# Reordering one product, one conversion, the value loads and one solve step in the first pass of a DeltaNet and maxout kernel

## The chip, the cores and the metric

The kernel runs on one core of a Trainium2 chip. The metric is the device time of one execution in microseconds (us); less is better. Besides the times there is one profiled execution, from which the trace and its page come. The engines are called as the page does: PE is TensorE (PEld its weight loads), DVE is VectorE, ACT is ScalarE, POOL is GpSimd, and SP only issues DMAs.

## What is computed

The reference has two layers. The first is the delta rule over 4 batches, 8 heads, 768 tokens and 48 dimensions; the second is a feed-forward layer that takes the maximum of three products.

```python
for t in range(S):                       # first layer; k_n are normalized keys
    kt, vt, bt = (k_n[:, :, t], v[:, :, t], beta[:, :, t, None])
    y[:, :, t] = np.einsum('bhd,bhde->bhe', q[:, :, t], state)
    v_old = np.einsum('bhde,bhd->bhe', state, kt)
    state = state + bt[:, :, :, None] * np.einsum('bhd,bhe->bhde', kt, vt - v_old)
...
h = np.maximum(np.maximum(x @ w1, x @ w2), x @ w3)   # second layer, x is y as 3072 x 384
return (h @ w_out).astype(np.float32)
```

The weights arrive as 64-bit words and are converted to 32-bit floats on the chip.

## The kernel before

**Tiles and stages.** The 768 tokens are cut into 12 chunks of 64. A chunk `c` consists of two units `n = 2c` and `2c + 1`, which hold two batches each. Two chunks make a group `m`, and a group is 512 rows of the feed-forward layer. For each group the kernel solves a triangular system (on VectorE), runs the recurrence of its two chunks (small matmuls on TensorE with copies between them), and puts the outcome through the feed-forward layer (large matmuls on TensorE). The feed-forward layer of group `m` is a generator, `ffn(m)` (L915), and work for the next groups is woven in between its steps.

**The order is written by hand.** Scheduling is manual (L96), so each engine does its instructions in the order in which the Python code issues them, and each DMA queue is in order too. The change concerns the loop over `ffn(0)` (L1141). Step `i` of this generator is one product of three matmuls with a hidden tile; the body of the loop then issues what belongs behind step `i`. Steps 0 to 17 are 256 columns wide (three tiles `f` in two halves, three products each), steps 18 to 26 are 512 wide, and steps 27 to 30 are the output products L958. In each three steps, the first is copied to `h` by ScalarE (L934), and the other two are joined to it by a maximum on VectorE (L940). These evictions free the two PSUM buffers `ffn` that the products take in turn.

**Pieces that the change touches**, with their short names in the tables `FIRST` (L1097) and `EARLY_LINKS` (L1090):

- `P4` to `P7` are key-query products of units 4 to 7: `gram(n, (1,))` (L427). The matmuls L438 fill one of three PSUM buffers called `two`, and a mask L422 on VectorE takes the outcome into `pt`.
- `z0`, `z1` are `join_z` (L702) for chunks 2 and 3 when called at i = 18: matmuls L709 and four copies L712 and L714 on ScalarE into `z`. `j0`, `j1` are `join_u` (L716): matmuls L723 that read `z`, and negated copies L683 into `ut`. `u0` is `new` (L762): matmuls L768 that read `ut` and the values. Their PSUM tiles come from the same three buffers `two`.
- `y1`, `s1` at i = 5 and 6 are the output and the state of chunk 1: on VectorE an addition L812 into `y` and an addition L798 into `st`. `T4` to `T7` turn query tiles on TensorE (L361), and `x1` turns `y`.
- `some(solving, n)` issues n steps of the triangular solve of group 1; a step is a multiplication L565 and a subtraction L569 on VectorE, with up to 256 elements a partition.
- `some(conv, 1)` issues one call of the weight conversion (L221): three operations on ScalarE (L238 to L240) for one piece, and for the piece of the call before a shift on VectorE (L250) and an addition on GpSimd (L254). Two buffers `mant` and `up` are taken in turn, so ScalarE's conversion waits for the addition of two pieces before. `fetch` (L211) loads the pieces, and `less_first` (L880) takes one set of weights from the two others (L883).
- `load_v(c)` (L136) loads the values of a chunk with two DMAs on SP's queue into one of three buffers; `prep_values(c)` (L292) scales them in place on GpSimd (L287). `old_k` (L747) later subtracts a product from them (L752). `load_q(n)` (L133) loads a query tile into one of three buffers with two DMAs.

At i = 16 and 17 units 10 and 11 write their key products to DRAM over GpSimd's queue (`at_d`, L468), and at i = 18 they are read back as `x_bl` (L515) for the solve of group 2, which begins at i = 20.

Of the kernel before, what the change touches and what calls it, by code (L numbers as in the profile page):

```python
# [23 lines left out]
def kernel(  # L24
# [84 lines left out]
    def rows(bb):  # L109
        return slice(C * bb, C * (bb + 1))  # L110
# [19 lines left out]
    def load_k(n, queues=one_queue):  # L130
        load(k, kpad[place(n)], n, queues)

    def load_q(n, queues=one_queue):  # L133
        load(q, qpad[n % NQ], n, queues)

    def load_v(c, queue=nc.sync):  # L136
        vts[c] = work.tile([128, 2, H, D], FP32, name="v_t", bufs=3)
        for bb in range(2):
            queue.dma_start(  # L139
                out=vts[c][rows(bb)].rearrange("p g h d -> p (g h) d"),  # L140
                in_=v[2 * bb : 2 * bb + 2, :, c * C : (c + 1) * C, :].rearrange(
                    "b h p d -> p (b h) d"
                ),
            )
# [66 lines left out]
    def fetch(queue=nc.scalar):  # L211
        if fetched[0] < len(pieces):
            _, src, (a, b) = pieces[fetched[0]]
            st = work.tile([128, 2 * 384], U32, name="w_bits", bufs=5)
            queue.dma_start(
                out=st.rearrange("p (a b) -> p a b", a=a), in_=src
            )
            staged.append(st)
            fetched[0] += 1
# [66 lines left out]
    def scale(c, nrm):  # L286
        nc.gpsimd.tensor_tensor(  # L287
            out=vts[c], in0=vts[c],
            in1=nrm[:, :, :, None].to_broadcast([128, 2, H, D]), op=ALU.mult,
        )  # L290

    def prep_values(c):  # L292

        if c in nrms:
            scale(c, nrms.pop(c))
# [84 lines left out]
    def load_blocks(n, queue=nc.gpsimd):  # L380
        c, g = divmod(n, 2)
        for i in range(2):
            if n % 4 == 2:
                t = kmore[i].rearrange("p a h d -> p (a h d)")[:, 0 : 2 * TURNED]
                t = t.rearrange("p (b x) -> p b x", b=2)
            else:
                t = work.tile(
                    [128, 2, TURNED], FP32, name="turned", tag="w_bits", bufs=5
                )
            turned[n, i] = t  # L390
            nc.gpsimd.memset(t[:, :, TURNED - 48 : TURNED], 0.0)  # L391
            for bb in range(2):
                for par in range(2):
                    for db in range(2):
                        p0, at = DP * par + 32 * db, 32 * (1 - db)
                        (queue, nc.gpsimd)[i].dma_start(  # L396
                            out=t[p0 : p0 + 32, bb, at : at + NP * 2 * D].rearrange(
                                "p (j x) -> p j x", j=NP
                            ),
                            in_=(k, q)[i][  # L400
                                2 * bb + g, :, c * C : (c + 1) * C, :
                            ].rearrange(
                                "(j two) (r tb) d -> two r j (tb d)", two=2, tb=2
                            )[par],
                        )
# [104 lines left out]
    def blocks(m):  # L510
        if m == 1:
            xs[m] = in_wo(0)
        else:
            xs[m] = work.tile([128, 2, HB * BL + HB], FP32, name="x_bl", bufs=1)
        nc.sync.dma_start(  # L515
            out=in_rows(xs[m]),
            in_=at_d[m].rearrange("c f b h j i -> (c f b h) j i"),
        )
# [361 lines left out]
    def less_first(f):  # L880
        part = (slice(None), slice(None), slice(f * 128, (f + 1) * 128))
        for i in (1, 2):
            nc.vector.tensor_tensor(  # L883
                out=w_sb[i][part], in0=w_sb[i][part], in1=w_sb[0][part],
                op=ALU.subtract,
            )

    def turn_first(fs):
        p_f = ps_two("p_t")
        for i, f in enumerate(fs):  # L890
            for t in range(KT):
                nc.tensor.transpose(
                    p_f[:, i, t * 128 : (t + 1) * 128],
                    w_sb[0][:, t, f * 128 : (f + 1) * 128],
                    ident,
                )
        for i, f in enumerate(fs):
            nc.scalar.copy(
                w_sb[0][:, :, f * 128 : (f + 1) * 128],
                p_f[:, i, 0 : KT * 128].rearrange("p (t x) -> p t x", t=KT),  # L900
            )
# [70 lines left out]
    def some(gen, n):  # L972
        for _ in range(n):
            if next(gen, gen) is gen:
                break

    conv = weights()
    solving = solve(0)
# [96 lines left out]
    for n in (2, 3):  # L1075
        masked(pts[n], by_par(pts[n]))
    load_q(4)
    load_v(2)
    solving = solve(1)
    some(solving, 1)  # L1080

# [15 lines left out]
    FIRST = {  # L1097
        0: "f1 s0 S1 S1", 1: "z1 d1 S1 k1 S1 S1", 2: "j1 S1 S1 S1",
        3: "S1 q1 S1 S1", 4: "u1 T4", 5: "y1", 6: "s1 T5", 7: "x1 T6",
        8: "T7", 14: "P4", 15: "P5", 21: "P6", 22: "P7",  # L1100
    }


# [11 lines left out]
    def links(m, names):  # L1115
        for name in names.split():
            f, i = name[0], int(name[1])
            if f in RECURS and m < GROUPS:
                RECURS[f](2 * m + i)
            elif f in MADE and m + 1 < GROUPS:  # L1120
                MADE[f](2 * (m + 1) + i)
            elif f in UNIT and m + 1 < GROUPS:
                UNIT[f](4 * (m + 1) + i)
            elif f == "N" and m + 2 < GROUPS:
                load_blocks(4 * (m + 2) + i)

    def queries(names):
        for name in names.split():
            f, n = name[0], int(name[1])
            if f not in OF_KEYS:  # L1130
                links(0, name)
                continue
            OF_KEYS[f](n)
            if f == "T" and n + 3 < 11:
                load_q(n + 3)
# [3 lines left out]
    CONVERTED = {*range(6), *range(11, 25)}  # L1139
    FETCHED = {8: 1, 12: 1, 13: 1, 14: 1, 18: 2, 19: 2, 20: 1, 21: 1}  # L1140
    for i, _ in enumerate(ffn(0)):  # L1141
        if 0 < i < 7:
            fetch(nc.sync)
        for _ in range(FETCHED.get(i, 0)):
            fetch(nc.gpsimd)
        if i in (18, 25):
            some(conv, 1)
        if i == 20:
            solving = solve(2)
            some(solving, 1)  # L1150
        if i == 21:
            some(solving, 3)
        queries(FIRST.get(i, ""))
        links(1, EARLY_LINKS.get(i, ""))
        if i in CONVERTED and i != 18:
            some(conv, 1)
        if 3 < i < 14:
            some(solving, (2, 1, 2, 2, 3, 3, 3, 3, 2, 2)[i - 4])
        if i in (5, 7):
            prep_values(i // 2)  # L1160
        if i in (1, 7):
            for n in range(2):
                load_k(8 + 2 * (i > 1) + n, (nc.gpsimd, nc.gpsimd))
        if i == 0:
            load_v(3)
        if i in (0, 2):
            load_q(5 + i // 2)
        if i == 11:
            load_q(11, (nc.gpsimd, nc.gpsimd))
        if i in (10, 21):  # L1170
            load_v(4 + i // 21)
        if i == 18:
            blocks(2)
        if i == 23:
            prep_values(4)
        if i > 21:
            some(solving, (3, 2, 3, 2, 2, 5, 5, 5, 4)[i - 22])
        if i in (27, 28, 29):
            load_blocks(i - 15, nc.sync)
        if i in (15, 17, 19, 22, 25, 27):  # L1180
            less_first((15, 17, 19, 22, 25, 27).index(i))
        if 27 <= i < 30:
            turn_first((2 * (i - 27), 2 * (i - 27) + 1))
# [5 lines left out]
    for m in range(1, GROUPS):  # L1189
        for i, _ in enumerate(ffn(m)):  # L1190
# [4 lines left out]
            if m + 2 < GROUPS:  # L1195
                if i == 6:
                    blocks(m + 2)
                if i == 8:
                    solving = solve(m + 2)
# [32 lines left out]
```

## Time and profile before

| what | us |
|---|---|
| median of 3 runs (lowest, highest) | 525.5 (524.5, 526.3) |
| profiled execution | 524.22 |
| its span, from first to last instruction | 522.5 |

The profiled execution is thus 1.7 us longer than its span. The granted clock of TensorE was 0.966 of full speed on the mean. Busy time by stretch of the span, in us (the engines work side by side, so the rows don't add up):

| stretch | what runs | PE | DVE | ACT | POOL | PE clock |
|---|---|---|---|---|---|---|
| 50 to 65 | i = 0 to 2 | 12.03 | 13.88 | 7.98 | 3.29 | 0.75 |
| 65 to 80 | i = 3 to 7 | 13.83 | 14.52 | 11.10 | 9.14 | 1.00 |
| 80 to 92 | i = 8 to 11 | 10.60 | 11.32 | 3.70 | 5.31 | 1.00 |
| 92 to 102 | i = 12 to 15 | 10.00 | 9.43 | 7.18 | 5.98 | 1.00 |
| 102 to 117 | i = 16 to 19 | 13.24 | 14.01 | 11.39 | 12.30 | 1.00 |
| 117 to 150 | i = 20 to 26 | 33.00 | 30.24 | 16.62 | 15.93 | 1.00 |
| 200 to 350 | later passes | 149.66 | 99.64 | 34.79 | 77.97 | 1.00 |

A stretch in which an engine is busy for its whole length is one that this engine may set the pace of. Short instructions leave a few hundredths of a microsecond between them, so 14.5 of 15 us on VectorE is as good as full.

### The profile page before, as it was taken

To read this page: it belongs to the slowest core of one execution; us is meant where nothing else is said; L and a number is where in the kernel's file an instruction comes from. 1 tells how busy PE (TensorE), PEld (TensorE's weight loads), DVE (VectorE), ACT (ScalarE), POOL (GpSimd) and SP (SyncE) were. 2 spreads that over 40 slices of the span, in tenths; PEclk is the share of its full clock that TensorE was granted. 3 is DMA by queue.
4 is the path that set the end of the run, shared out by engine and by line. 5 is a ranking of instruction groups with operands and counts; after the bars stand their busy time and mean duration, and the time that the engine had idled before them with its cause. 6 is when DMAs were issued, how large, how long until landed. Compare 5 with 4: busy or idle time off the path is not lost.

```text
span 522.5 us, 18030 instructions
## 1 busy us (share of the span) xinstructions
PE 495.1 (95%) x7840; PEld 305.9 (59%) x7840; DVE 311.0 (60%) x695; ACT 164.4 (31%) x302; POOL 190.6 (36%) x314
## 2 busy tenths in 40 slices
PE   6667898989999999999999999999999999999996
PEld 6556686855666555665556565655655555554453
DVE  5876999998995441699652988645897221111100
ACT  5557473776513142200143200242101411011000
POOL 7515155684383844951394780502130000000000
PEclk9855899999999999999999999999999999999999
DMA  8974958476035953444585444823343202220011
GB/s 111 214 154 114 162 163 138 133 154 199 3 89 135 188 90 69 135 125 115 111 157 121 111 131 102 171 43 91 81 109 85 43 3 63 61 61 0 0 30 32
DMA packets 108671, 53.47 MB, mean 102 GB/s; under 512 B 91760, under 2 KB 102928, under 8 KB 108592
## 3 DMA queue, kind: packets, MB, share of 16 engines
q1 hardware_dynamic: 97840, 34.44, 32.3%
q0 software_dynamic: 8640, 17.49, 13.5%
q8 instruction: 62, 1.02, 0.9%
q10 hardware_dynamic: 2112, 0.39, 0.5%
q14 instruction: 17, 0.14, 0.1%
HBM read 39.17 MB, written 13.11 MB: 100 GB/s over the span
## 4 chain that ended last, share of the span: by engine, by line
PE 79%; DVE 12%; ACT 2%; DMA 2%; issue 1%; POOL 1%; SPq 1%; DVEq 0%; ACTq 0%; POOLq 0%
PE p_h L926 34%; PE p_o L958 26%; PE p_g L438 3%; DVE tmp L565 3%; PE p_m L906 2%; PE p_u L768 2%; PE p_y L810 2%; DVE wo_sb L569 2%; DMA kmore<-in_k_dram 2%; PE p_k L740 2%; PE p_j L723 2%; PE p_s L791 1%; PE p_q L740 1%; SPq L120 1%; PE p_z L709 1%
## 5 line engine op out<-in xcount | busy, mean ns | idle before, releaser
L926 PE MATMUL p_h<-xt,w_sb 128*128 128x512 f32 (+1 forms) x522 | 218.9, 564 | 2.8 <-DVE h L940 1.3
L926 PEld LDWEIGHTS p_h<-xt,w_sb 128*128 128x128 f32 x522 | 96.1, 193 | 88.2 <-issue 79.5
L958 PE MATMUL p_o<-wo_sb,h 128*128 128x384 f32 x288 | 97.8, 489 | 0.0
L940 DVE TENSOR_TENSOR h<-h,p_h 128x512 f32<-128x512 f32 (+1 forms) x48 | 29.6, 617 | 90.0 <-PE p_h L926 89.9
L958 PEld LDWEIGHTS p_o<-wo_sb,h 128*128 128x128 f32 x288 | 53.7, 190 | 35.7 <-issue 0.5
L565 DVE TENSOR_TENSOR tmp<-x_bl,y_bl 128x31 f32<-128x31 f32 (+20 forms) x139 | 51.7, 372 | 4.1
L964 ACT COPY o_sb<-p_o 128x384 f32<-128x384 f32 x24 | 11.5, 479 | 134.2 <-PE p_o L958 128.1
L569 DVE TENSOR_TENSOR y_bl<-y_bl,tmp 128x31 f32<-128x31 f32 (+20 forms) x139 | 48.5, 349 | 4.8
L936 ACT ACTIVATE h<-p_h 128x512 f32<-128x512 f32 x30 | 17.9, 597 | 87.7 <-PE p_h L926 84.8
L958 PE MATMUL p_o<-w_sb,xt 128*128 128x384 f32 x120 | 42.0, 486 | 0.0
L396 POOL DMA_DIRECT2D turned<-in_q_dram x72 | 39.1, 551 | 3.9 <-POOL turned L391 2.9
L438 PE MATMUL p_g<-kqt 48*64 48x64 f32 (+1 forms) x1216 | 27.5, 239 | 6.8 <-DVE nt_bl L263 3.8
L438 PEld LDWEIGHTS p_g<-kqt 48*64 48x64 f32 x1216 | 24.3, 139 | 14.8 <-ACT kqt L367 8.0
L958 PEld LDWEIGHTS p_o<-w_sb,xt 128*128 128x128 f32 x120 | 22.8, 190 | 15.9
L120 POOL DMA_DIRECT2D kpad<-in_k_dram x32 | 21.8, 689 | 15.8 <-PE p_s L791 14.3
L287 POOL TENSOR_TENSOR v_t<-v_t,nrm 128x768 f32<-128x768 f32 x12 | 18.2, 1518 | 24.9 <-DVE nrm L266 12.1
L254 POOL TENSOR_TENSOR w_sb<-mant,up 128x384 int32<-128x384 int32 x18 | 18.3, 1018 | 24.3 <-DVE mant L250 21.7
L798 DVE TENSOR_TENSOR st<-st,p_s 48x768 f32<-48x768 f32 (+1 forms) x18 | 17.1, 949 | 15.0 <-PE p_s L791 14.8
L422 DVE TENSOR_TENSOR pt<-p_g,mask 128x512 f32<-128x512 f32 x20 | 13.7, 688 | 15.8 <-PE p_g L438 15.8
L139 POOL DMA_DIRECT2D v_t<-in_v_dram x12 | 9.9, 827 | 35.9 <-PE p_u L768 35.9
L391 POOL MEMSET turned<- 128x96 f32 x18 | 3.3, 191 | 44.8 <-DVE kqt L412 44.8
L768 PEld LDWEIGHTS p_u<-v_t,ut 64*64 64x64 f32 x768 | 13.5, 141 | 7.8 <-issue 7.3
(153 smaller groups left out, 624.5 us busy)
## 6 DMA issues: line engine op xcount, KB each, us to landing
w_bits<-in_moe_w_dram SPq DMA_DIRECT2D x14, 384.0 KB
out_dram<-o_sb SPq DMA_DIRECT2D x48, 96.0 KB
turned<-in_q_dram POOLq DMA_DIRECT2D x72, 48.0 KB, 2.9
kpad<-in_k_dram POOLq DMA_DIRECT2D x32, 96.0 KB, 4.9
y_x<-y SPq DMA_DIRECT2D x16, 192.0 KB
qall<-y_x SPq DMA_DIRECT2D x32, 96.0 KB
ut<-y_d SPq DMA_DIRECT2D x40, 64.0 KB
v_t<-in_v_dram SPq DMA_DIRECT2D x12, 192.0 KB
```

What stands on the lines that cost most here:

```text
L120: queues[bb].dma_start(out=dst[rows(bb ^ g), :, 0:D], in_=src[2 * bb + g, :, c * C : (c + 1) * C, :].rearrange("h p d -> p h d"),)
L254: nc.gpsimd.tensor_tensor(out=dst.bitcast(I32), in0=mant_v.bitcast(I32), in1=up_v, op=ALU.add)
L287: nc.gpsimd.tensor_tensor(out=vts[c], in0=vts[c], in1=nrm[:, :, :, None].to_broadcast([128, 2, H, D]), op=ALU.mult,)
L396: (queue, nc.gpsimd)[i].dma_start(out=t[p0 : p0 + 32, bb, at : at + NP * 2 * D].rearrange("p (j x) -> p j x", j=NP), in_=(k, q)[i][2 * bb ...
L438: nc.tensor.matmul(p_g[rows(bb ^ (g * i)), par, c0 : c0 + C * (1 + whole)], kq[:, 0], kq if whole else kq[:, i],)
L565: nc.vector.tensor_tensor(out=t_v, in0=row.to_broadcast(t_v.shape), in1=column.to_broadcast(t_v.shape), op=ALU.mult,)
L569: nc.vector.tensor_tensor(out=rest, in0=rest, in1=t_v, op=ALU.subtract)
L768: nc.tensor.matmul(p_v[rows(bb ^ g), g, i], ut[c % NU][rows(bb), g, h], rhs[rows(bb), g, h],)
L926: nc.tensor.matmul(p_h, w_sb[i][:, t, f * 128 : (f + 1) * 128], xt[:, t, lo : lo + w], start=(t == 0), stop=(t == KT - 1),)
L936: nc.scalar.activation(out=h, in_=p_h, func=mybir.ActivationFunctionType.Relu)
L940: nc.vector.tensor_tensor(out=h, in0=h, in1=p_h, op=ALU.max)
L958: nc.tensor.matmul(p_o, stays, moves, start=(n == 0), stop=(n == len(terms) - 1))
```

## The change

Four places of the loop over `ffn(0)` and the lines ahead of it are edited:

1. The key-query product of unit 5, `P5`, is issued at i = 19 (ahead of `j0`) and no longer at i = 15.
2. The conversion call of i = 18 is issued behind the links of that step (`d0 d1 z0 z1`) and no longer ahead of them.
3. The values of chunks 2 and 3 are loaded at i = 3 and i = 8 and no longer ahead of the loop and at i = 0; they are scaled at i = 8 and 12 and no longer at i = 5 and 7. The query tiles of units 5 and 6 are loaded at i = 1 and 3 and no longer at i = 0 and 2.
4. At i = 4 one step of the solve is issued and no longer two, and at i = 11 four and no longer three. So from i = 5 to i = 11 each output, state and eviction on VectorE stands one solve step further ahead.

No instruction is added or removed.

```diff
     load_q(4)
-    load_v(2)
     solving = solve(1)
...
-        8: "T7", 14: "P4", 15: "P5", 21: "P6", 22: "P7",
+        8: "T7", 14: "P4", 19: "P5", 21: "P6", 22: "P7",
...
-        if i in (18, 25):
+        if i == 25:
             some(conv, 1)
...
         queries(FIRST.get(i, ""))
         links(1, EARLY_LINKS.get(i, ""))
-        if i in CONVERTED and i != 18:
+        if i in CONVERTED:
             some(conv, 1)
         if 3 < i < 14:
-            some(solving, (2, 1, 2, 2, 3, 3, 3, 3, 2, 2)[i - 4])
-        if i in (5, 7):
-            prep_values(i // 2)
+            some(solving, (1, 1, 2, 2, 3, 3, 3, 4, 2, 2)[i - 4])
+        if i in (8, 12):
+            prep_values(i // 4)
...
-        if i == 0:
-            load_v(3)
-        if i in (0, 2):
+        if i in (1, 3):
             load_q(5 + i // 2)
         if i == 11:
             load_q(11, (nc.gpsimd, nc.gpsimd))
-        if i in (10, 21):
-            load_v(4 + i // 21)
+        if i in (3, 8, 10, 21):
+            load_v((3, 8, 10, 21).index(i) + 2)
```

## The prediction

> **What bounds the kernel now.** I read the page first (parts 1 and 2), then the chain of waits from 50 to 125 us, then the timelines of the engines over the same stretch. All of the change lies in the first feed-forward pass (i = 0 at 51 us to i = 30 at 166 us) and in the loads issued just ahead of it.
>
> ```profile
> PE 495.1 (95%) x7840; PEld 305.9 (59%) x7840; DVE 311.0 (60%) x695; ACT 164.4 (31%) x302; POOL 190.6 (36%) x314
> ...
> PE   6667898989999999999999999999999999999996
> ...
> DVE  5876999998995441699652988645897221111100
> ```
>
> A slice is 13 us. From slice 9 on TensorE is at nine tenths or more, so any microsecond that it gains before about 117 us should reach the end, unless a later wait takes it. Before that VectorE is the full one. The chain of waits (start, us, what) shows where it changes hands:
>
> ```profile
> 77.81 1.11 DVE wo_sb L569
> 78.92 0.86 DVE st L798
> 79.78 0.76 DVE tmp L565
> ...
> 80.56 1.59 DVE wo_sb L569
> ...
> 91.23 0.43 DVE h L940
> ...
> 91.71 1.56 PE p_h L926 x6
> ...
> 113.08 1.02 POOL w_sb L254
> 114.12 0.56 ACT mant L238
> ...
> 115.70 0.42 ACT z L712
> 116.15 0.59 ACT z L714
> ...
> 116.78 0.74 PE p_j L723 x49
> ```
>
> Three stretches: VectorE alone from 50.3 to 91.7; TensorE from 91.7 to 101.8; then a relay of VectorE, GpSimd's `at_d` writes, one weight addition (L254), one conversion on ScalarE (L238 to L240) and only then the copies of z, which release the joins on TensorE. TensorE's timeline shows the price as idle time in brackets:
>
> ```profile
> 60.05 0.21 PE L709 MATMUL p_z<-ut,at 32*32 32x32 f32 x1 [1.93 <-issue]
> 79.83 0.65 PE L361 MATMUL p_t<-ident,qall 128*128 128x128 f32 x4 [1.17 <-DVE st L798]
> 83.54 1.53 PE L926 MATMUL p_h<-xt,w_sb 128*128 128x256 f32 x6 [1.32 <-DVE h L940]
> 116.17 0.24 PE L723 MATMUL p_j<-z,t 32*32 32x32 f32 x2 [1.36 <-ACT z L712]
> 116.78 0.74 PE L723 MATMUL p_j<-z,t 32*32 32x32 f32 x62 [0.36 <-ACT z L714]
> ```
>
> The last four sum to 4.21 us, the most that these edits can reach. The first, 1.93 us, lies where VectorE is full and sets the pace: gaining it gives nothing.
>
> **What the Trainium skill says.** "SBUF — State Buffer", section "Who interferes with whom": a VectorE instruction with two SBUF inputs contends with a GpSimd instruction that reads SBUF, and the loser blocks for the whole instruction. The trace agrees. While GpSimd scales values,
>
> ```profile
> 78.60 3.27 POOL L287 TENSOR_TENSOR v_t<-v_t,nrm 128x768 f32<-128x768 f32 x2
> ```
>
> the pair of the 255-element step takes 0.83 and 1.58 us where a pair three steps on takes 0.42 and 0.42, while the state addition L798, one of whose inputs is PSUM, keeps 0.94 us. "Runtime: NRT & Kernel Launch", section "Instruction fetch mechanics": an engine's program comes in 16 KiB blocks over its own DMA queue; the page here has 62 packets and 1.02 MB on the instruction queue, so 16 KB each. One falls into 57 to 58 us, with the DMA engines at their fullest, beside the 1.93 us stall. "TensorE: Matmul & The Clock Gate", section "What's actually happening": an idle window brings half clock. Here the granted clock is 0.66 from 60.2 to 65.2 us, after that stall.
>
> **Part 1, values later and one solve step later (i = 4 to 12).** The step that leaves i = 4 and comes back at i = 11 puts the output L812 and the state L798 each one step earlier on VectorE: 0.42 + 0.42 us and two gaps of 0.02, 0.87 us. So the state ends about 0.87 sooner, of which the turn at 79.83 can use all: its gap of 1.17 falls to 0.3. Next, h L940 at 82.98 follows two further steps; without the scaling they lose 0.41 + 1.16 = 1.57 us of blocking. It would end near 81.0 and not 83.39, and TensorE, free at 81.3 by then, has no gap: 2.1 us ahead.
>
> But VectorE remains the bound. At i = 8 one scaling (1.65 us in the trace when it contends) now follows GpSimd's four kpad loads (2.73 us) and one weight fetch (0.78), so near 81.1 to 82.8, and meets solve steps. Not shown there; bound: nothing if it falls on a PSUM operation, 1.2 us (the larger block above) otherwise. I take 1.15, as VectorE does little else than steps then. Up to the eviction that ended at 91.65 VectorE is thus ahead by one step (192 elements, 0.36 + 0.36 + 0.05 = 0.77) + 1.57 - 1.15 = 1.2 us. TensorE's 2.1 is cut to 1.2.
>
> The step is paid back before the eviction at 98.64 to 99.05, which frees the buffer of the product of i = 15; that one started at 99.55, 0.5 us later. VectorE's lead there is 1.57 - 1.15 = 0.42, so TensorE's is at most 0.92. The second scaling at i = 12 comes behind the addition of 97.67 to 98.67; what follows on VectorE is one eviction and two masks from PSUM, which it does not block, and a `mant` shift (0.35, seen at up to 1.41 us when blocked). The next eviction has 3 us in hand, so I charge nothing; without that cover it is 1.1. Part 1: **0.9 us** (0 to 2.1).
>
> The loads themselves: the two value loads (two DMAs of 192 KB each) and two query loads move back on SP's queue. SP goes in order, so the weight fetches of i = 1 to 3 come ahead of them and the query load of i = 3 waits for the buffer that the third fetch waits for (until about 68.8). The query tiles are turned at 76 and 79.8, the values scaled at 81 and 98: the slack is 5 us or more. On GpSimd the kpad loads leave 3.3 us sooner. Cost nothing. The second scaling lands in GpSimd's densest stretch: 94 to 107.5 has 4.3 us idle (the brackets of its timeline), 2.27 of it in one piece ahead of the `at_d` writes, so 1.65 fits.
>
> **Part 2, key-query product from i = 15 to 19.** 32 matmuls, 0.69 us, and one mask of 0.68 us. On TensorE moved, not removed; it makes everything between 101 and 115 us 0.69 earlier and now fills the place ahead of the joins. The mask leaves the start of the relay at 101.80; the next shift waits for ScalarE until 102.4, so the relay gains little more than part 1's 0.42.
>
> **Part 3, conversion behind the copies of z (i = 18).** Before, ScalarE copied the hidden tile (112.29 to 112.88), waited 1.25 us for GpSimd's addition, converted for 1.5 us (114.12 to 115.6), then copied z in four pieces of 0.58. After, z follows the hidden copy. The relay up to there gains 0.4, so the first two copies end near 113.6. TensorE arrives: product of i = 19 ended at 114.81; less 0.92 and 0.69, plus 0.69 for the moved product, gives 113.9. So no wait: 1.36 + 0.36 = **1.72 us**. The conversion now stands ahead of the negated copies L683 (1.2 us), for which p_u waits: z ends near 115, conversion 116.5, L683 117.7; TensorE is through the second join at about 118.1. Slack 0.4. If GpSimd's addition (end near 114) is over 0.4 + 1 us late, the wait returns at p_u.
>
> Sum: 0.92 + 1.72 = 2.6 us. What is late next: from 120 VectorE is full again until 164, but its evictions end 2.3 to 5 us before TensorE needs their buffers, and the recurrence's p_u at 138.26 has 2.4. VectorE starts the next solve when ScalarE has taken the root, about 1.5 earlier, not 2.6; the 1.1 is inside that slack.
>
> Against the profiled execution (span 522.5, 524.2 with what lies around it) this gives 521.6; the median of the runs is 525.5, so **522.9**.
>
> **Rivals.**
> 1. Scaling still costs VectorE what it did (block of 1.2 at i = 8 and the 1.1 at i = 12 uncovered): part 1 gives 0, part 3 stays. For it: VectorE has no idle from 50 to 101. Against: the PSUM operations around i = 12. 525.5 - 1.7 = 523.8.
> 2. The wait moves from z to p_u: GpSimd's addition is late by the added 1.65, the conversion holds L683, and TensorE loses 1.2 to 2 at p_u. For it: ScalarE waited for that addition in both its last conversions (1.76 and 1.25). Against: the idle 2.27 on GpSimd. 522.9 + 1.6 = 524.5.
> 3. Slower: TensorE's stall on its own program falls, with other loads in flight, into 91 to 120 us, where nothing covers it. Place: the transfers of values now run beside weight fetches near 70 and 85 to 92 us. Price: 1.93, and half clock after it: p_h 2.80 for 1.56, p_k 1.53 for 1.15, a join 0.93 for 0.75, together 1.8; 3.7 in all. It decides once TensorE stands still for it, with the half clock counted, longer than the 2.6 us gained. Against: DMA share there is 0.4 to 1.05, at the stall it was 1.2 to 1.3. 522.9 + 3.7 = 526.6.
> 4. It does more: the scaling at i = 8 meets PSUM operations, and part 1 gives 2.1: 521.7.
>
> **How the numbers follow.** Forecast 0.50, rival 1 0.18, rival 2 0.14, rival 3 0.12, rival 4 0.06. A measurement of this kernel can tell 0.3%, 1.6 us (523.9 and 527.1). Faster takes the forecast, rival 4 and under half of rival 1: 0.62. Same: the rest of rival 1, rival 2, and half of rival 3: 0.27. Slower: 0.11, of rival 3 and what I haven't thought of. The range 521.0 to 526.4 reaches over rivals 1, 2 and 4 and leaves out rival 3; the forecast's own is 521.7 to 523.8.
>
> **What would show it.** Right: no gap of TensorE over 0.5 us at T6 and the product behind T7; the product of i = 12 about 1.2 sooner; joins directly behind the moved product, z's copies ahead of L238. Wrong: idle at p_u released by L683; TensorE waiting for h L940 at i = 15; an "issue" gap of over 1 us after 91 us; or all of it as told and a gap after 120 us that gives it back.

## The result and the profile after

The change made no difference that the measurement can tell: 526.35 us (median of 22 runs) where the kernel before has 525.23 (22 runs), a ratio of 1.0015 with a 95% interval from 0.9999 to 1.0031. Faster by 2.6 us had been forecast. The profiled execution took 526.12 us with a span of 524.3.

The page of the changed kernel, parts 1 and 2 (busy us by engine; busy tenths by slice):

```profile
PE 497.0 (95%) x7840; PEld 307.6 (59%) x7840; DVE 309.2 (59%) x695; ACT 164.4 (31%) x302; POOL 190.7 (36%) x314
...
PE   6667988989999999999999999999999999999996
...
DVE  5865999876997351599652988545897231111100
```

From slice 9 on the picture is as before. Its timeline of TensorE (start, us, ..., and in brackets the idle time ahead and who ended it) shows that the gaps have moved and not gone:

```profile
84.91 1.53 PE L926 MATMUL p_h<-xt,w_sb 128*128 128x256 f32 x6 [1.44 <-DVE h L940]
...
113.14 0.25 PE L709 MATMUL p_z<-ut,at 32*32 32x32 f32 x4 [0.85 <-DMA ut<-y_d]
113.56 0.72 PE L709 MATMUL p_z<-ut,at 32*32 32x32 f32 x60 [0.17 <-DMA ut<-y_d]
...
117.61 0.75 PE L723 MATMUL p_j<-z,t 32*32 32x32 f32 x64
...
127.28 1.15 PE L791 MATMUL p_s<-u,kmore 64*64 64x48 f32 x64 [0.96 <-ACT u L773]
```

The joins (L723) have no wait any more. In its place stand one wait for solved blocks, ahead of them, and one for `u`, behind them; and the gap at the product of i = 9 is still there.

To compare executions I count from the copy L877 on VectorE that opens the loop. It starts at 50.34 us in the execution of before and 51.83 in that of after. The engines do the same up to there (the lag of after is there at 38.8 us already, ahead of every edit), and in all fourteen profiled executions of this study it lies between 50.32 and 52.05, so 1.49 of the 1.8 us between the two spans is scatter. The rest, from there (us, worked out from the timelines of TensorE; each row is one execution, the waits are TensorE's idle time in brackets, and "its us" is how long the product of i = 19 took):

| kernel | first p_z | waits at p_z | product of i = 19 | its us | first join | p_u | wait at p_s | p_s | end |
|---|---|---|---|---|---|---|---|---|---|
| before | 60.09 | 0 | 61.63 | 2.84 | 65.83 | 70.56 | 0 | 75.00 | 472.16 |
| after | 59.70 | 1.02 | 62.38 | 2.84 | 65.78 | 69.91 | 0.96 | 75.45 | 472.47 |
| relay_only | 59.24 | 0.71 | 61.75 | 2.84 | 65.14 | 69.28 | 1.50 | 75.37 | 472.06 |
| values_only | 63.62 | 0 | 64.90 | 2.84 | 68.81 | 73.53 | 0 | 77.93 | 474.39 |
| values_back | 58.60 | 1.60 | 62.15 | 4.24 | 66.95 | 71.09 | 0 | 75.49 | 472.04 |
| root_behind | 59.70 | 1.64 | 63.35 | 5.49 | 69.49 | 73.63 | 0 | 78.03 | 475.55 |
| conv_only | 60.04 | 0 | 61.40 | 2.84 | 64.17 | 68.31 | 0 | 72.71 | 469.99 |
| conv_root | 60.08 | 0.59 | 62.36 | 2.84 | 65.13 | 69.27 | 0 | 73.67 | 472.19 |
| p5_back | 60.24 | 0.58 | 62.47 | 2.84 | 65.24 | 69.38 | 2.02 | 75.98 | 473.94 |
| scale_sooner | 58.71 | 1.77 | 62.15 | 4.48 | 67.18 | 71.32 | 0 | 75.72 | 472.29 |
| solve_sooner | 59.89 | 0.33 | 61.92 | 2.82 | 65.30 | 69.44 | 0.73 | 74.75 | 473.08 |
| step_only | 59.29 | 0.59 | 61.48 | 2.84 | 65.59 | 70.31 | 0 | 74.72 | 471.35 |
| conv_solve | 61.36 | 0 | 62.64 | 2.84 | 65.42 | 69.56 | 0 | 73.96 | 472.08 |
| best_b | 59.91 | 0 | 61.19 | 2.84 | 63.96 | 68.17 | 0 | 72.70 | 470.14 |

Between before and after: the product of i = 19 starts 0.75 later; from there to p_u 1.40 is gained (8.93 before, 7.53 after); from p_u to p_s 1.10 is lost (4.44, 5.54). In sum p_s is 0.45 later. The chain of waits of after (start, us, what) names the last of the three:

```profile
114.67 3.29 DMA at_d<-at
117.95 0.03 SPq L515
117.98 0.04 issue
118.02 6.90 DMA x_bl<-at_d
124.92 0.02 issue
124.94 0.03 ACT root_bl L261
...
126.43 0.81 ACT u L773
127.24 0.04 issue
127.28 1.15 PE p_s L791 x64
```

ScalarE stands at the root of the next solve, whose input is read back from DRAM, and the copy of `u` stands behind it.

### The profile page after: what moved, and what is told of

Its sections match the earlier page's. It is cut to its first block, busy times and chain, and to the rows that moved or that the text cites. A ratio compares the mean times of both kernels' runs of the same rounds, so it can differ in the third digit from the quotient of the medians.

```text
span 524.3 us, 18024 instructions
## 1 busy us (share of the span) xinstructions
PE 497.0 (95%) x7840; PEld 307.6 (59%) x7840; DVE 309.2 (59%) x695; ACT 164.4 (31%) x302; POOL 190.7 (36%) x314
## 4 chain that ended last, share of the span: by engine, by line
PE 81%; DVE 9%; ACT 3%; DMA 3%; issue 2%; POOL 1%; SPq 0%; ACTq 0%; DVEq 0%
PE p_h L926 34%; PE p_o L958 25%; PE p_g L438 5%; PE p_m L906 2%; PE p_y L810 2%; PE p_k L740 2%; PE p_u L768 2%; PE p_q L740 2%; PE p_s L791 2%; PE p_t L361 1%; DMA x_bl<-at_d 1%; PE p_j L723 1%; DVE wo_sb L569 1%; PE p_z L709 1%; DVE tmp L565 1%
## 5 line engine op out<-in xcount | busy, mean ns | idle before, releaser
L438 PE MATMUL p_g<-kqt 48*64 48x64 f32 (+1 forms) x1216 | 29.1, 247 | 6.6 <-DVE nt_bl L263 3.8
L438 PEld LDWEIGHTS p_g<-kqt 48*64 48x64 f32 x1216 | 25.8, 147 | 15.3 <-ACT kqt L367 7.8
L455 ACT COPY at<-p_g 128x512 f32<-128x512 f32 x21 | 12.3, 584 | 19.4 <-DVE pt L422 17.1
```

Of the source, the lines that this page charges most:

```text
L438: nc.tensor.matmul(p_g[rows(bb ^ (g * i)), par, c0 : c0 + C * (1 + whole)], kq[:, 0], kq if whole else kq[:, i],)
```

## Experiments

Each kernel was timed in five rounds beside the kernel before, which had medians of 524.83, 524.74 and 524.94 us in the three sets below. Ratios are to the kernel before, with a 95% interval; they are not the quotient of the two medians, and differ from it by up to 0.13% (solve_sooner: 0.9984 and 0.9997).

**First four: which part loses the gain.** Two theories stood against each other: V, that the moved scalings block VectorE for longer; R, that a wait further down the relay takes the place of the one at the joins.

relay_only:

```diff
-        8: "T7", 14: "P4", 15: "P5", 21: "P6", 22: "P7",
+        8: "T7", 14: "P4", 19: "P5", 21: "P6", 22: "P7",
...
-        if i in (18, 25):
+        if i == 25:
...
-        if i in CONVERTED and i != 18:
+        if i in CONVERTED:
```

> The kernel before with two of the four edits: the key-query product of unit 5 at i = 19 and the conversion of i = 18 behind the copies of z. Theory V (the moved scalings block VectorE for longer, about 3.4 us against 1.6, and so part 1 and everything that follows is lost): without them the 1.72 us at the joins is gained, 523.5 us where the kernel before has 525.2. Theory R (the relay: once z is early, the read-back of x_bl and the root on ScalarE, or the solved blocks ut, take the place of the wait): gain of 0.3 us at most, 524.9 or more, with TensorE idle at p_s or p_z in its profile.

Measured: 524.91 us, ratio 1.001 (0.9993 to 1.0028). No gain, as R says, though nothing of the values was moved. TensorE now waits at p_z for the landing of `ut`, and at p_s for `u` (timeline of relay_only):

```profile
111.01 0.25 PE L709 MATMUL p_z<-ut,at 32*32 32x32 f32 x4 [0.43 <-DMA ut<-y_d]
111.54 0.72 PE L709 MATMUL p_z<-ut,at 32*32 32x32 f32 x60 [0.28 <-DMA ut<-y_d]
...
125.81 1.15 PE L791 MATMUL p_s<-u,kmore 64*64 64x48 f32 x64 [1.50 <-ACT u L773]
```

The second wait is the larger: `x_bl` landed 7.6 us after its issue, and the root, behind which the copy of `u` stands, waited for it.

values_only:

```diff
     load_q(4)
-    load_v(2)
...
-        if i in (5, 7):
-            prep_values(i // 2)
+        if i in (8, 12):
+            prep_values(i // 4)
...
-        if i == 0:
-            load_v(3)
-        if i in (0, 2):
+        if i in (1, 3):
             load_q(5 + i // 2)
...
-        if i in (10, 21):
-            load_v(4 + i // 21)
+        if i in (3, 8, 10, 21):
+            load_v((3, 8, 10, 21).index(i) + 2)
```

> The kernel before with the later loads and scalings of the values (and the two query loads one or two steps later) alone. Theory V: slower by 0.5 to 1.5 us, near 526.2, with a solve step beside the first scaling stretched to 2 us or more, and the last step of the solve 0.4 us or more later against the start of the loop. Theory R: no difference, 525.2.

Measured: 526.46 us, ratio 1.0038 (1.0023 to 1.0053): slower, as V says. So both theories hold, each for its part. Timeline of values_only, VectorE and GpSimd beside each other:

```profile
80.67 1.58 DVE L565 TENSOR_TENSOR tmp<-wo_sb 128x256 f32<-128x256 f32 x1
...
81.33 0.78 POOL L215 DMA_DIRECT2D w_bits<-in_moe_w_dram  x1
...
82.13 1.49 POOL L287 TENSOR_TENSOR v_t<-v_t,nrm 128x768 f32<-128x768 f32 x1
82.28 1.63 DVE L569 TENSOR_TENSOR wo_sb<-wo_sb,tmp 128x256 f32<-128x256 f32 x1
```

Two operations that take 0.42 us each when alone take 1.58 and 1.63. The first ends when the weight fetch ahead of the scaling does, the second when the scaling does. So the fetch counts too: 2.4 us for one scaling. In this execution a second loss follows: TensorE waited 2.10 us at the product of i = 9, and its clock was at half from 85.3 to 92.1 us.

values_back is the changed kernel without the lines of values_only.

> The changed kernel with loads and scalings of the values (and the two query loads) where the kernel before has them. Theory V: the gain that was forecast for the rest, 523.0 us. Theory R: about 525.0, with the wait for x_bl on ScalarE and for u on TensorE still there.

Measured: 525.72 us, ratio 1.0018 (1.0002 to 1.0035). V alone falls: TensorE reaches the first p_z 1.1 us sooner than in after (58.60, 59.70), and nothing comes of it. The wait for `u` at p_s, which R expected, isn't there in this execution; the wait for `ut` has grown to 1.60 us, and the product behind it takes 4.24 us and not 2.84. Busy time by stretch of values_back (us and counts by engine, then the granted clock of TensorE, DMA share, GB/s):

```profile
111.00:113.00 2.00, 1.47 (x65) 1.33 (x66) 1.07 (x3) 2.00 (x5) 2.00 (x4) 0.76 0.54 80
113.00:115.00 2.00, 2.00 (x3) 0.79 (x3) 0.00 (x0) 1.95 (x4) 1.99 (x4) 0.50 0.16 33
115.00:117.00 2.00, 2.00 (x16) 0.67 (x18) 0.04 (x1) 1.68 (x4) 1.98 (x4) 0.88 0.82 270
```

The clock is at half behind the wait. This is what the Trainium skill, "TensorE: Matmul & The Clock Gate", section "What's actually happening", says of an idle TensorE. The page puts it at an idle window of about 3.4 us or more; here it came with one idle stretch of 1.60 us between the small matmuls of p_z. But 1.50 us of idle at p_s in relay_only left the clock at 1.00, so the length of one wait doesn't decide it, and these runs don't show what does.

root_behind moves the start of the next solve, in the changed kernel, behind the joins of i = 20:

```diff
-        if i == 20:
-            solving = solve(2)
-            some(solving, 1)
...
         links(1, EARLY_LINKS.get(i, ""))
+        if i == 20:
+            solving = solve(2)
+            some(solving, 1)
```

> The changed kernel with the start of the solve of group 2 (the root on ScalarE, which waits for x_bl) issued behind the second join and p_u of i = 20 and not ahead of them. Both theories: the idle 0.96 us of TensorE ahead of p_s goes, as u no longer stands behind the root: 525.4 us where the changed kernel has 526.35. Theory R says that nothing else stood in the way, so that TensorE has no other gap after 100 us; theory V that the gap at p_z (1.0 us, solved blocks late) stays.

Measured: 526.25 us, ratio 1.003 (1.0015 to 1.0045). The idle time at p_s is gone (p_u to p_s 4.40, after 5.54), the time isn't better: a miss of both theories. In this execution, which took 529.45 us and so lies far above the median, the waits at p_z were 1.35 us (put down by the profile to ScalarE's L238, which p_z doesn't read) and 0.29, and the clock stayed at half for the whole next product (windows of root_behind, columns as above):

```profile
115.00:117.00 2.00, 2.00 (x35) 1.17 (x27) 0.00 (x0) 1.95 (x5) 1.99 (x3) 0.50 0.38 65
117.00:119.00 2.00, 2.00 (x4) 0.70 (x3) 0.00 (x0) 1.98 (x4) 1.98 (x4) 0.50 0.56 184
119.00:121.00 2.00, 2.00 (x11) 0.50 (x12) 0.01 (x1) 0.05 (x1) 0.62 (x2) 0.50 0.92 267
```

Theory W came from this: in the four executions with the product at i = 19 the second half of p_z starts 61.0 to 62.4 us behind the start of the loop, when `ut` has landed, and TensorE was already there. The key-query product at i = 15 would be the cover that kept it from waiting.

**Second four: the cover, the root, the scalings.** conv_only is the kernel before with the two `conv` edits of relay_only and without the line of `P5`.

> The kernel before with the conversion of i = 18 behind the copies of z alone; the key-query product stays at i = 15. Theory W (the product at i = 15 was cover: without its 0.69 us TensorE reaches the second p_z before the solved blocks ut have landed, stands still 0.7 to 1.6 us, and in some executions runs at half clock for the next product): no wait at p_z and no half clock here, joins directly behind the product of i = 19, so that u0 is 1.7 us sooner against the start of the loop; then p_s waits for u behind the root (up to 1.5 us), and the time is 524.0 to 524.8 us. Theory R alone (x_bl and the root take it all): 524.8, as relay_only.

Measured: 523.31 us, ratio 0.9979 (0.9965 to 0.9992), faster than before and, with relay_only at 1.001 (0.9993 to 1.0028), apart from it by the place of that product alone (the two were timed in different sets, each against the kernel before). Its timeline of TensorE:

```profile
111.15 1.43 PE L709 MATMUL p_z<-ut,at 32*32 32x32 f32 x128
112.51 2.84 PE L926 MATMUL p_h<-xt,w_sb 128*128 128x512 f32 x6
115.28 0.75 PE L723 MATMUL p_j<-z,t 32*32 32x32 f32 x64
115.96 2.84 PE L926 MATMUL p_h<-xt,w_sb 128*128 128x512 f32 x6
118.74 0.75 PE L723 MATMUL p_j<-z,t 32*32 32x32 f32 x64
119.42 1.19 PE L768 MATMUL p_u<-v_t,ut 64*64 64x48 f32 x64
```

There is no bracket from p_z to p_u. The expected wait for `u` did not come, either: `x_bl` landed 4.9 us after its issue, and p_s started 2.3 us sooner than before (72.71, 75.00).

conv_root is conv_only with the edit of root_behind.

> As conv_only, and the start of the solve of group 2 behind the second join and p_u of i = 20. Theory W with R as its second wait: both waits gone, the 1.7 us stay, 523.1 us (before 524.8), and TensorE has no gap after 101 us in its profile. If something further limits, 524.5 or more.

Measured: 524.31 us, ratio 0.9986 (0.9969 to 1.0004); not 523.1. A miss: at p_s there was nothing to gain (4.40 us from p_u to p_s in both executions). There are two new gaps. One is 0.59 us at p_z for `ut`, though the product is at i = 15: the cover doesn't always suffice. The other is at the next place that reads VectorE, as the solve that starts later holds up L752 there (timeline of TensorE, conv_root):

```profile
138.77 1.15 PE L768 MATMUL p_u<-v_t,ut 64*64 64x48 f32 x64 [1.00 <-DVE v_t L752]
```

p5_back is the changed kernel with `15: "P5"` in the table again.

> The changed kernel with the key-query product of unit 5 back at i = 15. Theory W: the wait at p_z goes and with it the half clock behind it, so faster than the changed kernel (526.35) by 0.5 to 1.5 us, near 525.4. Rival (the waits at p_z come from the later solve, 0.45 us, and not from the product): the wait at p_z stays at 0.3 us or more.

Measured: 524.25 us, ratio 0.9994 (0.9973 to 1.0014), some 0.2% under after, with intervals that overlap. The wait at p_z fell from 1.02 to 0.58 us and did not go: the rival has a part in it, since with the moved scalings the last solve step ends later (48.91 us behind the start of the loop, 48.40 before). In this execution `x_bl` landed 7.9 us after its issue, p_s waited 2.02 us for `u`, and the clock was at half for the 3.4 us after that.

scale_sooner puts the scalings elsewhere in the changed kernel:

```diff
-        if i in (8, 12):
-            prep_values(i // 4)
+        if i in (7, 10):
+            prep_values(i // 3)
```

> The changed kernel with the scalings at i = 7 (ahead of the four kpad loads and the weight fetch on GpSimd) and i = 10 (in GpSimd's idle stretch). Theory B (a scaling that stands directly behind a fetch on GpSimd blocks VectorE through the fetch too, 0.8 and 1.5 us, just ahead of the eviction that TensorE waits for): no solve step over 1.7 us, the gap of 1.4 us at the product of i = 9 under 0.5, VectorE ahead by 1.0 us or more at the last solve step, 0.5 to 1.5 us faster than the changed kernel. Rival (any scaling beside solve steps costs about 2 us in all): the gap stays and so does the time.

Measured: 525.77 us, ratio 1.0013 (0.9998 to 1.0029). The mechanism is as B says: the first scaling stands directly behind an addition and meets the state from PSUM, no solve step is over 1.6 us, and the gap of 1.44 us at the product of i = 9 is gone; the last solve step comes 0.7 us sooner, where 1.0 had been expected. The time isn't better; its execution shows what that of values_back showed: 0.36 and 1.41 us of wait for `ut`, and 4.48 us for the product behind it.

**Last four: the landing of ut, one part left, and combinations.** solve_sooner is the changed kernel with

```diff
-            some(solving, (1, 1, 2, 2, 3, 3, 3, 4, 2, 2)[i - 4])
+            some(solving, (1, 1, 2, 2, 3, 3, 3, 6, 1, 1)[i - 4])
```

so that the write `y_d` of the solved blocks stands ahead of the four `at_d` writes of i = 12 on SP's queue.

> The changed kernel, and the last solve step and the write of the solved blocks (y_d) of group 1 at i = 11, the first read of ut at i = 12: six solve calls at i = 11 and one each at i = 12 and 13. Theory W (the wait at p_z is for the landing of ut): ut lands 1.5 us or more sooner, the wait at p_z and the half clock behind it go, and the time is 525.0 us where the changed kernel has 526.35; the wait for u behind the root (1 us) may stay. Rival (the wait at p_z is not worth more than its own 0.3 to 1 us, or the order of DMAs makes ut no sooner): 526.0 or more.

Measured: 524.79 us, ratio 0.9984 (0.9971 to 0.9997), against 1.0015 (0.9999 to 1.0031) for after: the intervals just fail to touch. Its queue of SP shows the new order:

```profile
98.59 1.14 SPq L591 DMA_DIRECT2D y_d<-wo_sb  x2
99.82 3.07 SPq L468 DMA_DIRECT2D at_d<-at  x4
102.99 7.83 SPq L600 DMA_DIRECT2D ut<-y_d  x8
```

From the start of the loop `y_d` is issued at 47.37 and not 49.96, and the wait at p_z is 0.33 us and not 1.02. The forecast of a landing 1.5 us sooner did not come true: SP issues the eight reads one after the other, the last of them only 0.9 sooner (58.33, 59.24), and the second half of p_z starts 0.5 sooner (61.25, 61.73). A wait of 0.73 us at p_s stays. This execution was the slowest of its 22 (526.0 us) and ends no sooner than that of after, so the profile doesn't show where the time of the others was gained.

step_only is the kernel before with the line of `some(solving, ...)` as in the change.

> The kernel before with one solve step moved from i = 4 to i = 11 alone. The forecast's own term for it (0.77 us for VectorE up to the eviction of i = 10, paid back before that of i = 13): TensorE turns a query tile 0.9 us sooner at T6, the product of i = 12 starts about 0.8 sooner against the start of the loop, that of i = 15 at most 0.5 sooner, and the joins wait as before: 524.3 to 524.8 us, which is no difference.

Measured: 525.19 us, ratio 1.0007 (0.9992 to 1.0022), no difference, as expected, though above the times named. The gap at T6 falls from 1.17 to 0.25 us and a gap of 0.59 for `ut` appears: TensorE reaches the first p_z 0.80 sooner than before and the product of i = 19 only 0.15 sooner.

conv_solve is conv_only with `(2, 1, 2, 2, 3, 3, 3, 5, 1, 1)` for the solve; best_b is the changed kernel with the edits of p5_back, scale_sooner and solve_sooner together.

> The kernel before with the conversion of i = 18 behind the copies of z, and the end of the solve of group 1 (last step and write of y_d at i = 11, reads of ut at i = 12 and 13) sooner. Theory W: as conv_only or better, 522.8 to 523.4 us, without a wait at p_z.

> The changed kernel with the three places mended that the runs before pointed to: the key-query product back at i = 15, the scalings at i = 7 and 10, the end of the solve at i = 11 to 13. Theory W and B together: both gaps at T6 and the product of i = 9 gone, no wait at p_z, joins without a wait: 522.0 to 523.0 us. If the wait for u behind the root (x_bl late) takes over: 524 or more, with that gap in its profile.

Measured: conv_solve 523.84 us, ratio 0.9981 (0.9963 to 0.9998), from six runs; best_b 524.05, ratio 0.9992 (0.9971 to 1.0013). Neither adds to conv_only, and both lie above the times expected. The profiled execution of best_b has no wait at p_z, at the joins or at p_s and ends 470.14 us behind the start of the loop, 2.0 sooner than before, but its 14 runs lie between 522.0 and 528.7, and I did not find out why.

## Why the prediction was wrong

**The step that failed** is in part 2: the moved product "makes everything between 101 and 115 us 0.69 earlier and now fills the place ahead of the joins". It begins right (the product of i = 16 starts 51.50 us behind the start of the loop and not 52.25). But between 101 and 115 us stands p_z, which reads `ut`, and the landing of `ut` was put at nothing in the sum. At the first p_z 0.39 of the gain is left (0.29 of it went to a wait for ScalarE's copy of `h` at i = 17), TensorE waits 1.02 there, and the product of i = 19 starts 0.75 later than before; then the moved product costs its 0.69 again.

The wait is longer than the 0.39, so `ut` was late as well: the last of its eight reads was issued 59.24 us behind the start of the loop, and 57.60 before. Of these 1.64 the solve, which ended 0.44 later, explains a part. The rest varies from one execution to the next: in relay_only, where the solve ended as before, the last read was issued at 58.62.

All six executions with the product at i = 19 wait at p_z, 0.33 to 1.77 us; of the eight with it at i = 15 three wait, 0.58 or 0.59. By times, moving it costs the difference between conv_only (0.9979) and relay_only (1.001), 0.31% (estimated from the two intervals, 0.1 to 0.5%), 1.6 us. How the 1.6 come about is not shown: in the two executions 0.97 is lost up to p_u, by the work at its new place and the wait, and 1.69 more up to p_s, where `u` waits behind the root for `x_bl`. That the wait at p_z is worth something by itself is supported by solve_sooner, where only the end of the solve, and with it the order of the DMAs behind it, is changed.

**Part 3 had the mechanism right.** The copies of z came ahead of the conversion and both waits, 1.36 and 0.36 us, went. Alone (conv_only) it is worth 0.21% (0.08 to 0.35%), 1.1 us, of the 1.72 forecast.

**Part 1 was mis-sized**, 0.9 forecast, 0 measured (the product of i = 15 starts 49.21 and 49.23 us behind the start). The one solve step did what was said (step_only: T6 0.9 sooner). The block by the first scaling was taken as 1.15 us and at a place behind the eviction of i = 7. It was 2.4, and ahead of it (timeline of after):

```profile
81.64 2.80 DVE L569 TENSOR_TENSOR wo_sb<-wo_sb,tmp 128x255 f32<-128x255 f32 x1
81.86 0.78 POOL L215 DMA_DIRECT2D w_bits<-in_moe_w_dram  x1
...
82.65 1.49 POOL L287 TENSOR_TENSOR v_t<-v_t,nrm 128x768 f32<-128x768 f32 x1
```

One subtraction of 0.42 us lasted over fetch and scaling, so the gap at the product of i = 9 stayed, 1.44 us. The second scaling was charged nothing; the shift beside it took 1.34 us and not 0.35. Before, the two scalings in a row cost 1.57 together, as the first ran beside the state from PSUM. And a late solve is not only late evictions: it is a late `ut`. The move of the values alone is slower by 0.38% (values_only), where the forecast had VectorE 0.42 us ahead by it; in the profiled execution the half clock adds to the block.

**What is late next** named the evictions and the p_u at 138.26. It had the root only as the start of the next solve, 1.5 us sooner, and not as a wait for a DMA with the copy of `u` behind it. In the execution of after the root came 73.1 us behind the start of the loop where it had been 70.3, as `x_bl` was issued 1.4 later and landed 6.9 us after its issue. That cost the 0.96 at p_s, the second place where the gain at the joins was lost.

**The rivals.** Rival 1 (part 1 gives nothing) was true as far as it went. Rival 2 had a wait behind the joins in the right engine, but at p_u and for GpSimd's addition; it came at p_s and for a DMA. Rival 3, a stall on TensorE's own program behind 91 us, did not show in the execution of after; its half clock did, in four others (values_back, root_behind, scale_sooner, p5_back), behind other waits. Rival 4, that part 1 gives more, did not come. The chances have a slip: the parts named for "same" (0.12, 0.14 and 0.06) sum to 0.32 and not to 0.27.

**What stays open.** `x_bl` landed between 4.9 us (conv_only) and 7.9 us (p5_back) after its issue, 6.9 in after. GpSimd issues five weight fetches at the same time, but its place among them doesn't explain the spread: in conv_only it was issued 1.0 us ahead of the third fetch, in solve_sooner 1.3, and there it took 6.8. So what part of the loss at p_s belongs to the change is not known. That the executions of after without a long wait at p_z are the faster ones is likely and not shown, since only one of them was profiled.

## What to carry to other kernels

Before pulling work ahead of a wait, look for the next input with its own clock, here blocks that come back through DRAM; if its landing coincides with the time at which they are used, what is gained upstream is lost there (step_only: 0.65 of 0.80 us), and work that is moved from ahead of it to behind it is paid again. Moving the source of the wait helped the changed kernel (solve_sooner) but added nothing where no wait was left (conv_solve). And what a GpSimd operation costs VectorE depended on what stood beside it and what stood in the queue ahead of it (1.57 us for two scalings before, 2.4 for one after), so such a price can't be carried from one place to another.

## What the runs showed of the hardware

A solve operation with two SBUF inputs was blocked while GpSimd issued a weight fetch that a scaling stood directly behind (1.58 us for 0.42), though a fetch without one behind it, at 84.53 us in the kernel before, left the operation at 84.68 at 0.42 us. Why was not tried.

The length of a single wait of TensorE did not decide whether half clock followed. It did after 1.35 to 1.60 us at p_z (values_back, root_behind, scale_sooner), after 2.02 at p_s (p5_back) and after 2.10 at the product of i = 9 (values_only); it did not after 1.36 at the joins (before), 1.44 at the product of i = 9 (after) and 1.50 at p_s (relay_only). By the clock records of the traces, each stretch of half clock that began behind 54 us, in all fourteen executions, lasted 3.41 or 6.83 us, so its price comes in fixed pieces; at half clock the product of 2.84 us took up to 5.49.
